# Two dense layers behind local and strided attention on one core: score blocks of 32 queries, and probabilities transposed two blocks at a time

## The chip, the cores and the metric

One core of a Trainium2 chip runs the whole program in one launch. The metric is the device time of one execution in microseconds (us), lower is better. The engines are TensorE (PE in the profile, its weight loads PEld), VectorE (DVE), ScalarE (ACT), GpSimd (POOL) and SyncE (SP), which here only issues DMAs.

## What is computed

Attention of 4 batches x 8 heads with 576 positions and head size 64, then two dense layer pairs on the 2304 tokens of 512 features, all in fp32 (the dense layers as sums of rounded products):

```python
rel = pos[:, None] - pos[None, :]
mask_local = (rel >= 0) & (rel < 32)                                # heads 0..3
mask_strided = (rel >= 0) & (pos[None, :] % 32 == pos[:, None] % 32)  # heads 4..7
scores = np.where(mask, q @ k.T / 8, -1e9)
attn = softmax(scores); x = attn @ v
...
h = x @ w_in;  g = where(h >= 1, h, where(h <= -1, 0, (h + 1) ** 2 / 4));  x = g @ w_out
h = x @ w_in2; r = max(h, 0); out = (s * r * r + b) @ w_out2
```

A local query sees itself and the 31 keys before it. A strided query sees the keys before it that are a multiple of 32 away, so 18 positions of equal residue form one small causal problem.

## The kernel before

**Units.** Attention is cut into 16 units, one for each batch and pair of heads; unit `b_p` is batch b, pair p, and pairs 0 and 1 are local, 2 and 3 strided. The two heads of a pair (index `a`) lie in the two halves of the 128 partitions. A unit loads q and k (`load_qk`) and v (`load_v`), transposes q and k (`trans`), forms scores in two PSUM banks (`scores`), takes the softmax (`smax`, `sscale`, `sexp`, `ssum`, `smul`), transposes the probabilities on TensorE (`ptrans`), copies them to SBUF on ScalarE (`evac_p`), multiplies with v (`pv`) and copies the output into `xr` (`evac_o`).

**Blocks before (lines 38 and 39).** A local unit has 9 blocks of 64 queries and 96 keys, a strided one 11 blocks of 54 queries and 54 keys (three residues of 18 positions). A bank of scores first gets the mask, as a bf16 matmul with the identity over all 128 partitions; then each block adds one fp32 matmul per head, `s<-qk,qk` in the trace. `ptrans` makes one 128-row transpose per block (`p<-ident,s`). `pv` multiplies one block of one head at a time (`o<-pt,v`): weights are v, 64 columns wide; what streams are the 64 or 54 queries of the block. A strided v is loaded with 3 DMAs per head, a local one with 2 and a fill.

**Dense layers.** They make up most of TensorE's work: `h<-xh,w`, `h<-xl,w` (first layer of a pair) and `y<-g,w`, `y<-w,g` (second). Weights are split on ScalarE, VectorE and POOL into a rounded part and a rest (`c`, `wc`, `w`) as they arrive, and so is x (`x_split`: `xh`, `xl`).

**Order.** `attention_moe_moe` does not issue instructions; it records them with a planned time (`PACE`, `STARTS`, `PASSES`), and `Order.issue` replays them by its own prices, engine by engine, into the order that stands in the program: of the ready operations of an engine the one with the earliest planned time goes next. The pieces of attention thereby stand among dense matmuls. During the start it puts filler matmuls (`idle<-u`) on TensorE. The first four units (batch 0, `QUICK`) take a shorter path, load v by POOL's queue and borrow memory (tiles named `mem`); the other twelve load v by SP's queue.

Of the kernel before, what the change touches and what calls it, by code (L numbers as in the profile page):

```python
# [19 lines left out]
P = 128  # L20
# [57 lines left out]
N_MASK_L = 2 * 96  # L78
N_MASK_S = 54
N_CONST = N_MASK_L + N_MASK_S + P  # L80


def constants():

    row = np.arange(P)[:, None] % 64
    col = np.arange(96)[None, :]
    back = row - (col - 32)
    local = np.where((back >= 0) & (back < STRIDE), 0, DROP).astype(np.float32)
    first = np.where(col < 32, DROP, local).astype(np.float32)
# [3 lines left out]
    return np.ascontiguousarray(  # L93
        np.concatenate([first, local, strided, np.eye(P, dtype=np.float32)], axis=1)
    )


class Order:
# [6 lines left out]
    def __init__(self, nc):  # L105
        self.nc, self.ops, self.place, self.count, self.seen, self.first = nc, [], {}, {}, {}, {}
        self.past = set()
        self.filler = []
        self.choices, self.uses = {}, {}
        self.tiles, self.shadow = {}, bacc.Bacc("TRN2", target_bir_lowering=False, num_devices=1)  # L110
        self.now = self.earliest = 0.0
        for e in self.ENGINES:
            setattr(self, e, Order.Engine(self, e))
# [56 lines left out]
    def record(self, engine, op, args, kw):  # L170
# [191 lines left out]
def attention_moe_moe(ctx, tc, q, k, v, w1_in, w1_out, w2_in, w2_out, s_in, b_in, consts, out):  # L362
# [42 lines left out]
    class Unit:  # L405
# [31 lines left out]
        def trans(self, w):  # L437
            if w == 0:
                self.qk = [self.mem["qk"][x](f"qk{x}_{self.id}") for x in range(2)]
            o = self.qk[w][:, PAD:PAD + S]  # L440
# [19 lines left out]
        def load_v(self):  # L460
# [3 lines left out]
            for a in range(2):  # L464
                t = self.mem["v"][a](f"v{a}_{self.id}")
                if self.strided:
                    t = t[:54, :11 * D].rearrange("p (i d) -> p i d", d=D)
                    src = vh[a].rearrange("(t r) d -> t r d", r=STRIDE)
                    for r in range(3):
                        n = 11 if r < 2 else 10  # L470
                        queue.dma_start(out=t[r * NPOS:(r + 1) * NPOS, :n], in_=src[:, r:r + 3 * (n - 1) + 1:3])
                else:
                    t = t[:96, :9 * D].rearrange("p (i d) -> p i d", d=D)
                    nc.gpsimd.memset(t[:32, 0], 0.0)
                    win = vh[a]
                    ap = bass.AP(tensor=win.tensor, offset=win.offset + 32 * D, ap=[[D, 96], [64 * D, 8], [1, D]])
                    queue.dma_start(out=t[32:96, 0], in_=win[:64])
                    queue.dma_start(out=t[:, 1:], in_=ap)
                self.v.append(t)

        def scores(self):
            qt, kt = self.qk
            if not self.strided:

                nc.gpsimd.memset(kt[:, :PAD], 0.0)
            self.sp = [bank(f"s{g}_{self.id}") for g in range(2)]
            i = 0
            for g in range(2):
                n, kw = self.s_split[g], self.kw
                first = not self.strided and g == 0  # L490
                bk = self.sp[g][:, :n * kw].rearrange("p (i c) -> p i c", c=kw)
                mask = mask_s if self.strided else mask_l[:, kw:]
                if first:
                    nc.tensor.matmul(bk[:, 0], ident_b, mask_l[:, :kw], start=True, stop=False, skip_group_check=True)
                nc.tensor.matmul(
                    bk[:, first:], ident_b, mask.unsqueeze(1).to_broadcast([P, n - first, kw]), start=not first, stop=False,
                    skip_group_check=True,
                )
                for c in range(n):
                    for a in range(2):  # L500
                        r = slice(64 * a, 64 * a + 64)
                        if self.strided:
                            r0, r1 = RES * i, min(STRIDE, RES * i + RES)
                            m, kn = NPOS * (r1 - r0), NPOS * (r1 - r0)
                            of, by = [x[r, PAD + NPOS * r0:PAD + NPOS * r1] for x in (qt, kt)]
                        else:
                            m, kn = 64, self.kw
                            of, by = qt[r, PAD + 64 * i:PAD + 64 * i + 64], kt[r, 64 * i:64 * i + self.kw]
                        nc.tensor.matmul(
                            self.sp[g][64 * a:64 * a + m, c * self.kw:c * self.kw + kn], of, by,  # L510
                            start=False, stop=True, skip_group_check=True,
                        )
# [14 lines left out]

        def sscale(self):

            if self.quick:  # L530
                self.s = self.mem["s"](f"s_{self.id}")[:, :self.nb * self.kw].rearrange("p (i c) -> p i c", c=self.kw)
# [11 lines left out]
        def sexp(self):  # L543
# [4 lines left out]
            self.s = self.mem["s"](f"s_{self.id}")[:, :self.nb * self.kw].rearrange("p (i c) -> p i c", c=self.kw)  # L548
# [20 lines left out]
        def ptrans(self, part):  # L569
            i0, i1 = ((0, 8), (8, self.nb))[part]  # L570
            if part == 0:
                self.pt = [
                    self.mem["p"][x](f"pt{x}_{self.id}")[:self.kw, :n * P].rearrange("p (i c) -> p i c", c=P)
                    for x, n in enumerate((8, self.nb - 8))
                ]
            self.pb[part] = []
            for j in range(i0, i1, 4):
                n = min(4, i1 - j)
                bk = bank(f"p{j}_{self.id}")
                for i in range(j, j + n):  # L580
                    nc.tensor.transpose(bk[:self.kw, (i - j) * P:(i - j + 1) * P], self.s[:, i, :], ident)
                self.pb[part].append((j, n, bk))

        def evac_p(self, part):
            for j, n, bk in self.pb[part]:
                nc.scalar.activation(
                    out=self.pt[part][:, j - 8 * part:j - 8 * part + n],
                    in_=bk[:self.kw, :n * P].rearrange("p (i c) -> p i c", c=P),
                    func=AF.Copy,
                )  # L590

        def pv(self):
            self.ob = [bank(f"o{g}_{self.id}") for g in range(2)]
            i = 0
            for g in range(2):
                for c in range(self.o_split[g]):
                    n = min(self.qw, S - self.qw * i)
                    kn = n if self.strided else self.kw
                    for a in range(2):
                        nc.tensor.matmul(  # L600
                            self.ob[g][64 * a:64 * a + 64, c * self.qw:c * self.qw + n],
                            self.v[a][:kn, i],
                            self.pt[i // 8][:kn, i % 8, 64 * a:64 * a + n],
                            start=True, stop=True,
                        )
                    i += 1

        def evac_o(self, copy):

            x = x_raw(self.b)[:, self.pair]  # L610
            i0 = 0
            for g in range(2):
                i1 = i0 + self.o_split[g]
                c0, c1 = self.qw * i0, min(S, self.qw * i1)
                o = self.ob[g][:, :c1 - c0]
                if self.strided:
                    put(
                        self.b, copy, x.rearrange("p (t r) -> p r t", r=STRIDE)[:, c0 // NPOS:c1 // NPOS],
                        o.rearrange("p (r t) -> p r t", t=NPOS),
                    )  # L620
                else:
                    put(self.b, copy, x[:, c0:c1], o)
                i0 = i1
# [173 lines left out]
    def room(tag, width):  # L797
# [3 lines left out]
        raw=[room("raw0", 6 * P), room("raw1", 6 * P)], qk=[room("qp0", 8 * P), room("qp1", PAD + S)], s=room("as", 864),  # L801
        p=[room("qp0", 8 * P), room("qp1", PAD + S)], v=[room("v0", 11 * D), room("v1", 11 * D)],
    )
# [134 lines left out]
```

## Time and profile before

| | us |
|---|---|
| median of 3 runs | 936.61 |
| lowest, highest | 935.33, 937.09 |
| profiled execution | 936.63 |
| its span, first to last instruction | 934.8 |
| mean granted TensorE clock | 0.995 |

| engine | busy us | share of the span |
|---|---|---|
| PE | 921.9 | 99% |
| PEld | 866.4 | 93% |
| DVE | 413.1 | 44% |
| ACT | 382.8 | 41% |
| POOL | 295.9 | 32% |

Matmuls overlap, so a row of the timeline gives the start of a group, the time to its modelled end, and its count; what a group costs is read from its start to the start of the next. An fp32 matmul of scores or values leaves two records, so counts of `s` and `o` are twice those of the program. The last attention unit ends near 360 us; the rest of the span is dense layers alone.

### The profile page before, as it was taken

How to read it: one execution, taken by the hardware profiler on the slowest of the kernel's cores; microseconds unless marked ns; L12 is line 12 of the kernel's file. 1: busy time of each engine (PE TensorE's matmuls, PEld its weight loads, DVE VectorE, ACT ScalarE, POOL GpSimd, SP SyncE). 2: the span in 40 equal slices, each digit the busy share in tenths (PEclk: the TensorE clock that was granted, in tenths of full speed). 3: DMA queues.
4: the chain of work that ended last, by engine and by line, in shares of the span. 5: the costliest groups of instructions: out<-in, count | busy, mean ns of one | idle time of the engine just before them, and what ended most of it. 6: DMA issues, size and time to landing. Idle time of an engine off the chain costs nothing.

```text
span 934.8 us, 18580 instructions
## 1 busy us (share of the span) xinstructions
PE 921.9 (99%) x7744; PEld 866.4 (93%) x7744; DVE 413.1 (44%) x659; ACT 382.8 (41%) x853; POOL 295.9 (32%) x276
## 2 busy tenths in 40 slices
PE   8989999999999999999999999999999999999998
PEld 7889999999999999999999989999889999889997
DVE  2788875433334342224369996332323232222221
ACT  2777876544444443222356554222222222222221
POOL 6166554111121212222246665222222222222221
PEclk9989999999999999999999999999999999999999
DMA  9997233322322210001375910110102010000000
GB/s 160 293 288 265 69 90 85 67 39 46 62 45 62 45 61 22 1 23 70 117 258 180 320 74 2 46 46 1 46 1 69 4 66 1 23 1 23 1 23 23
DMA packets 107495, 72.77 MB, mean 78 GB/s; under 512 B 77372, under 2 KB 94184, under 8 KB 107412
## 3 DMA queue, kind: packets, MB, share of 16 engines
q1 hardware_dynamic: 106452, 70.14, 26.4%
q0 software_dynamic: 960, 1.45, 0.9%
q8 instruction: 61, 1.00, 0.5%
q14 instruction: 22, 0.18, 0.1%
HBM read 57.93 MB, written 13.63 MB: 77 GB/s over the span
## 4 chain that ended last, share of the span: by engine, by line
PE 96%; DMA 1%; ACT 1%; SPq 1%; POOL 0%; issue 0%; DVE 0%; POOLq 0%
PE h L358 44%; PE y L358 44%; PE s L358 3%; PE o L358 2%; PE p L358 2%; DMA mem<-in_k_dram 1%; PE idle L358 1%; SPq L358 1%; PE t L358 1%; POOL w L358 0%; ACT mem L358 0%; ACT c L358 0%; DVE xl L358 0%; POOL xl L358 0%; ACT qk L358 0%
## 5 line engine op out<-in xcount | busy, mean ns | idle before, releaser
L358 PE MATMUL h<-xh,w 128*128 128x256 f32 x2304 | 436.8, 282 | 0.1
L358 PEld LDWEIGHTS h<-xh,w 128*128 128x128 f32 x2304 | 364.8, 189 | 4.6 <-ACT w L358 0.3
L358 POOL TENSOR_TENSOR g<-u,g 128x512 fp32r<-128x512 f32 x144 | 189.5, 1316 | 506.2 <-ACT g L358 211.3
L358 PE MATMUL h<-xl,w 128*128 128x256 f32 x1152 | 324.4, 282 | 0.9 <-DVE xl L358 0.9
L358 PE MATMUL y<-g,w 128*128 128x256 f32 x1728 | 223.3, 282 | 0.0
L358 PEld LDWEIGHTS h<-xl,w 128*128 128x128 f32 x1152 | 217.7, 189 | 5.0 <-DVE xl L358 1.3
L358 PE MATMUL y<-w,g 128*128 128x512 f32 x864 | 212.3, 395 | 0.0
L358 PEld LDWEIGHTS y<-g,w 128*128 128x128 f32 x1728 | 210.1, 188 | 1.5
L358 PEld LDWEIGHTS y<-w,g 128*128 128x128 f32 x864 | 157.2, 188 | 32.4
L358 DVE SCALAR_TENSOR_TENSOR u<-h,u 128x512 f32<-128x512 f32 x72 | 49.7, 691 | 253.3 <-ACT u L358 253.3
L358 ACT ACTIVATE g<-u 128x512 fp32r<-128x512 f32 x144 | 90.9, 631 | 118.3 <-DVE u L358 117.6
L358 ACT ACTIVATE u<-h 128x512 f32<-128x512 f32 x72 | 43.1, 599 | 188.2 <-PE h L358 187.0
L358 DVE TENSOR_SCALAR u<-h 128x512 f32<-128x512 f32 x72 | 49.6, 690 | 143.8 <-PE h L358 139.6
L358 POOL TENSOR_TENSOR w<-wc,w 128x512 fp32r<-128x512 f32 x64 | 84.9, 1331 | 52.8 <-ACT w L358 47.9
L358 ACT ACTIVATE u<-u,half 128x512 f32<-128x512 f32 x72 | 51.9, 721 | 113.3 <-DVE u L358 109.6
L358 DVE TENSOR_TENSOR u<-h,u 128x512 f32<-128x512 f32 x72 | 49.3, 684 | 25.2 <-ACT u L358 25.2
L358 ACT ACTIVATE w<-wc 128x512 fp32r<-128x512 f32 x64 | 40.0, 627 | 15.2 <-DVE wc L358 15.1
L358 DVE TENSOR_SCALAR c<-c 128x512 int32<-128x512 int32 x64 | 42.9, 689 | 4.5 <-ACT c L358 4.5
L358 DVE SCALAR_TENSOR_TENSOR wc<-wr,c 128x512 int32<-128x512 int32 x64 | 42.7, 675 | 3.5 <-POOL w L358 3.2
L358 DVE SCALAR_TENSOR_TENSOR c<-wr,c 128x512 int32<-128x512 int32 x64 | 43.2, 686 | 0.3
L358 ACT ACTIVATE c<-wr 128x512 f32<-128x512 f32 x64 | 39.7, 630 | 7.9 <-DMA wr<-in_moe_w_out_dram 7.7
L358 DVE TENSOR_SCALAR u<-u,sbt 128x512 f32<-128x512 f32 x72 | 42.0, 584 | 1.7
(60 smaller groups left out, 514.9 us busy)
## 6 DMA issues: line engine op xcount, KB each, us to landing
wr<-in_moe_w_in_dram SPq DMA_DIRECT2D x32, 512.0 KB
wr<-in_moe_w_out_dram SPq DMA_DIRECT2D x32, 512.0 KB
x<-o SPq DMA_DIRECT2D x34, 256.0 KB
xr<-x SPq DMA_DIRECT2D x17, 512.0 KB
out_dram<-o SPq DMA_DIRECT2D x18, 256.0 KB
v<-in_v_dram SPq DMA_DIRECT2D x12, 192.0 KB
raw<-in_q_dram SPq DMA_DIRECT2D x32, 72.0 KB
raw<-in_k_dram SPq DMA_DIRECT2D x32, 72.0 KB
```

What stands on the lines that cost most here:

```text
L358: getattr(getattr(self.nc, engine), op)(*args, **kw)
```

## The change

Local blocks of 32 queries and 64 keys: 18 of them, two per score slot (`e`), so that a slot of 64 columns holds two blocks in the two 32-partition halves of a head; the mask has 64 columns. Probabilities lie at a pitch of 64 columns in both kinds of unit (a strided slot fills its 10 spare columns and the empty twelfth slot with zeros on VectorE), and `ptrans` transposes 128 columns, two slots, at once. A slot's transposed probabilities then lie in the upper or the lower 64 partitions, and v is loaded so that it matches: `pv` multiplies slot `i + x` with rows `64 x` on, into bank `ob[x]`. In `pv` the recorded matmuls are held to the written order (`in_line`). Output leaves in three copies instead of two. Strided v takes 6 DMAs per head, local v 3, and the two fills of zeros for keys before the first are gone.

```diff
-LOCAL = dict(nb=9, qw=64, kw=96, s_split=(5, 4), o_split=(8, 1))
-STRIDED = dict(nb=11, qw=54, kw=54, s_split=(6, 5), o_split=(9, 2))
-PAD = 32
+LOCAL = dict(nb=9, kw=64, s_split=(8, 1), cut=(4, 1))
+STRIDED = dict(nb=11, kw=54, s_split=(6, 5), cut=(4, 2))
+PITCH = 64
...
+def local_block(i, e):
+    return 2 * i + 1 if e else 2 * i + 2 if i < 8 else 0
...
+        if self.in_line and self.line is not None:
+            turn.add(self.line)
+        self.line = i if self.in_line else None
...
-                    t = t[:54, :11 * D].rearrange("p (i d) -> p i d", d=D)
+                    t = t[:, :6 * D].rearrange("p (i d) -> p i d", d=D)
                     src = vh[a].rearrange("(t r) d -> t r d", r=STRIDE)
-                    for r in range(3):
-                        n = 11 if r < 2 else 10
-                        queue.dma_start(out=t[r * NPOS:(r + 1) * NPOS, :n], in_=src[:, r:r + 3 * (n - 1) + 1:3])
+                    for r in range(6):
+                        n = len(range(r, STRIDE, 6))
+                        p = 64 * (r // 3) + r % 3 * NPOS
+                        queue.dma_start(out=t[p:p + NPOS, :n], in_=src[:, r::6])
                 else:
-                    nc.gpsimd.memset(t[:32, 0], 0.0)
...
-                    queue.dma_start(out=t[32:96, 0], in_=win[:64])
-                    queue.dma_start(out=t[:, 1:], in_=ap)
+                    queue.dma_start(out=t[:, :4], in_=vh[a][:512].rearrange("(i s) d -> s i d", s=P))
+                    queue.dma_start(out=t[:, 5:], in_=vh[a][32:544].rearrange("(i s) d -> s i d", s=P))
+                    queue.dma_start(out=t[:64, 4], in_=vh[a][512:])
...
+                    o = self.sp[g][:, c * kw:(c + 1) * kw]
+                    for e in range(1 if self.strided else 2):
+                        for a in range(2):
...
+                                t = 32 * local_block(i, e)
+                                m, kn, u = 32, kw, max(0, t - 32)
+                                of, by = qt[r, t:t + m], kt[r, u:u + kn]
+                            nc.tensor.matmul(
+                                o[64 * a + 32 * e:64 * a + 32 * e + m, :kn], of, by, start=False, stop=True, skip_group_check=True,
+                            )
...
+            if self.strided:
+                nc.vector.memset(t[:, :, self.kw:], 0.0)
+                nc.vector.memset(t[:, self.nb, :self.kw], 0.0)
...
+            w = P if self.strided or part == 0 else PITCH
+            bk = self.pb[part] = bank(f"p{part}_{self.id}")[:w, :cut * P]
+            for i in range(cut):
+                nc.tensor.transpose(bk[:, i * P:(i + 1) * P], self.double[:, part * self.cut[0] + i, :w], ident)
...
+            nc.in_line = True
+            for i in range(0, self.nb, 2):
+                for a in range(2):
+                    for e in range(1 if self.strided else 2):
+                        for x in range(min(2, self.nb - i)):
+                            if self.strided:
+                                n, at, j = min(54, S - 54 * (i + x)), 27 * i, i // 2
+                                kn = n
+                            else:
+                                n, at = 32, 32 * (i + 1 - e if i < 8 else i + e)
+                                j, kn = i // 2 if e else 5 + i // 2 if i < 8 else 0, 64
+                            r, c = slice(64 * x, 64 * x + kn), 64 * a + 32 * e
+                            nc.tensor.matmul(
+                                self.ob[x][64 * a:64 * a + 64, at:at + n], self.v[a][r, j], self.pt[i // 8][r, i // 2 % 4, c:c + n],
+                                start=True, stop=True,
+                            )
+            nc.in_line = False
```

**TensorE, values of strided unit 3_2.** Before, eight matmuls of the first output bank, three dense ones, and the next eight; `v_3_2_4000` and `v_3_2_4022` are v of the two heads:

```order
L358 MATMUL p_3_2_4250<-ident,s_2_4132 54x128 x4
L358 MATMUL p_3_2_4257<-ident,s_2_4132 54x128 x3
L358 MATMUL y_0_4108<-g_2_4139,w_4_1_1097 128x256 x2
L358 MATMUL o_3_2_4264<-pt_3_2_4253,v_3_2_4000 64x54
L358 MATMUL o_3_2_4264<-pt_3_2_4253,v_3_2_4022 64x54
...
L358 MATMUL o_3_2_4264<-pt_3_2_4253,v_3_2_4000 64x54
L358 MATMUL o_3_2_4264<-pt_3_2_4253,v_3_2_4022 64x54
L358 MATMUL y_0_4108<-g_2_4139,w_5_1_1188 128x256 x3
L358 MATMUL o_3_2_4264<-pt_3_2_4253,v_3_2_4000 64x54
L358 MATMUL o_3_2_4264<-pt_3_2_4253,v_3_2_4022 64x54
```

Dense matmuls stood between the blocks there. After, all 22 follow each other; the two banks `4501` and `4503` (upper and lower rows) alternate inside a head, and these are the last of them:

```order
L370 MATMUL o_3_2_4501<-pt_3_2_4497,v_3_2_4241 64x54
L370 MATMUL o_3_2_4503<-pt_3_2_4497,v_3_2_4241 64x54
L370 MATMUL o_3_2_4501<-pt_3_2_4497,v_3_2_4298 64x54
L370 MATMUL o_3_2_4503<-pt_3_2_4497,v_3_2_4298 64x54
L370 MATMUL o_3_2_4501<-pt_3_2_4497,v_3_2_4241 64x36
L370 MATMUL o_3_2_4501<-pt_3_2_4497,v_3_2_4298 64x36
L370 MATMUL y_0_4336<-g_2_4368,w_4_1_1089 128x256
L370 MATMUL y_0_4336<-g_2_4368,w_5_1_1168 128x256 x3
```

Of the twelve units of batches 1 to 3, values stood in three pieces in nine and in one or two in the others; after the change they stand in one piece, but for 1_0, 1_1, 1_2 (one matmul ahead of the rest) and 2_2 (16 and 6).

**POOL, start, softmax sums and loads of batch 0.** Before, all v loads stand ahead of the first softmax sum (`sm`):

```order
L358 DMA mem_1_201<-in_v_dram 18x11x64 x2
L358 DMA mem_1_201<-in_v_dram 18x10x64
L358 ISA
L358 TENSOR_SCALAR sm_0_304<-sm_0_304 128x9
L358 TENSOR_SCALAR sm_1_392<-sm_1_392 128x9
L358 TENSOR_SCALAR sm_3_512<-sm_3_512 128x11
L358 TENSOR_TENSOR xl_595<-xr_543,xh_584 128x512
L358 TENSOR_SCALAR sm_2_608<-sm_2_608 128x11
L358 TENSOR_TENSOR w_0_0_603<-wc_0_0_582,w_0_0_603 128x512
```

After, loads of strided v (`v_0_3`, `mem`) stand between the sums, and the last three behind the split of the first x (`xl_705`):

```order
L370 TENSOR_SCALAR sm_0_297<-sm_0_297 128x9
L370 DMA v_0_3_199<-in_v_dram 18x5x64 x2
L370 DMA mem_0_437<-in_v_dram 18x6x64 x2
L370 TENSOR_SCALAR sm_1_442<-sm_1_442 128x9
L370 DMA mem_0_437<-in_v_dram 18x5x64 x4
L370 DMA mem_1_599<-in_v_dram 18x6x64 x2
L370 DMA mem_1_599<-in_v_dram 18x5x64
L370 TENSOR_TENSOR xl_705<-xr_607,xh_688 128x512
L370 DMA mem_1_599<-in_v_dram 18x5x64 x3
L370 TENSOR_SCALAR sm_3_527<-sm_3_527 128x11
L370 TENSOR_SCALAR sm_2_669<-sm_2_669 128x11
L370 TENSOR_TENSOR w_0_0_676<-wc_0_0_656,w_0_0_676 128x512
```

What moved: `sm_3` now comes behind `xl_705` and twelve loads, `sm_2` behind three loads more; both are sums of strided units of batch 0.

## Rows read from the trace of the kernel before

**Rows 1.** The page, chain that ended last, share by engine.
```profile
PE 96%; DMA 1%; ACT 1%; SPq 1%; POOL 0%; issue 0%; DVE 0%; POOLq 0%
```

**Rows 2.** Stretches: length, busy us (count) by engine, granted clock, DMA share, GB/s.
```profile
50.00:60.00 10.00, 8.82 (x59) 7.77 (x59) 8.80 (x13) 7.01 (x15) 5.37 (x5) 0.66 0.98 267
...
120.00:360.00 240.00, 240.00 (x2524) 229.30 (x2525) 103.93 (x166) 122.20 (x373) 57.84 (x66) 1.00 0.27 60
```

**Rows 3.** Timeline, PE, 201.7 us: start, us to modelled end, operation, out<-in, count.
```profile
201.72 2.99 PE L358 MATMUL y<-g,w 128*128 128x256 f32 x24
204.55 0.28 PE L358 MATMUL h<-xh,w 128*128 128x256 f32 x1
```

**Rows 4.** Timeline, PE, scores of a local unit.
```profile
219.28 0.38 PE L358 MATMUL s<-narrow 128*128 128x96 bf16 x2
219.59 1.04 PE L358 MATMUL s<-qk,qk 64*64 64x96 f32 x20
220.56 0.34 PE L358 MATMUL s<-narrow 128*128 128x384 bf16 x1
220.83 0.88 PE L358 MATMUL s<-qk,qk 64*64 64x96 f32 x16
221.64 0.38 PE L358 MATMUL h<-xh,w 128*128 128x256 f32 x1
```

**Rows 5.** Timeline, PE, values of units 0_3 (o<-pt,v) and 0_2 (o<-mem,mem).
```profile
46.51 0.24 PE L358 MATMUL o<-mem,mem 54*64 54x54 f32 x1
46.53 0.22 PE L358 MATMUL o<-pt,v 36*64 36x36 f32 x1
46.59 0.41 PE L358 MATMUL o<-mem,mem 54*64 54x54 f32 x8
```

**Rows 6.** Timeline, PE, transposes and values of a strided unit.
```profile
209.50 1.36 PE L358 MATMUL p<-ident,s 128*54 128x128 f32 x11
210.61 0.48 PE L358 MATMUL y<-g,w 128*128 128x256 f32 x2
211.02 0.67 PE L358 MATMUL o<-pt,v 54*64 54x54 f32 x16
211.62 0.62 PE L358 MATMUL y<-g,w 128*128 128x256 f32 x3
...
213.91 0.54 PE L358 MATMUL o<-pt,v 54*64 54x54 f32 x12
214.39 0.39 PE L358 MATMUL h<-xl,w 128*128 128x256 f32 x1
```

**Rows 7.** Timeline, PE, values of a local unit in one piece.
```profile
141.54 1.27 PE L358 MATMUL o<-pt,v 96*64 96x64 f32 x36
142.74 0.51 PE L358 MATMUL y<-g,w 128*128 128x256 f32 x2
```

**Rows 8.** Timeline, PE, values of a local unit in three pieces, first and last.
```profile
330.79 0.27 PE L358 MATMUL h<-xh,w 128*128 128x256 f32 x1
331.00 0.69 PE L358 MATMUL o<-pt,v 96*64 96x64 f32 x16
...
333.35 0.39 PE L358 MATMUL h<-xl,w 128*128 128x256 f32 x1
333.58 0.39 PE L358 MATMUL h<-xh,w 128*128 128x256 f32 x2
```

**Rows 9.** Timeline, POOL, start.
```profile
7.31 2.00 POOL L358 DMA_DIRECT2D v<-in_v_dram  x3
...
34.29 0.21 POOL L358 TENSOR_SCALAR sm<-sm 128x11 f32<-128x11 f32 x1 [5.86 <-DVE sm L358]
38.43 1.30 POOL L358 TENSOR_TENSOR xl<-xr,xh 128x512 fp32r<-128x512 f32 x1 [3.93 <-ACT xh L358]
```

**Rows 10.** DMA issues by line: count, KB each, median us to landing.
```profile
v<-in_v_dram POOLq DMA_DIRECT2D x4, 49.5 KB, 7.9
```

**Rows 11.** Timeline, PE, dense matmuls after the start.
```profile
53.09 0.58 PE L358 MATMUL h<-xl,w 128*128 128x256 f32 x1 [0.89 <-DVE xl L358]
```

More of the change, by code (lines that the diff above doesn't have):

```diff
@@ L77 @@
 U_BUFS, WC_BUFS = 3, 2
-N_MASK_L = 2 * 96
+N_MASK_L = 2 * 64
 N_MASK_S = 54
 N_CONST = N_MASK_L + N_MASK_S + P
+def local_block(i, e):
+    return 2 * i + 1 if e else 2 * i + 2 if i < 8 else 0
 def constants():
     row = np.arange(P)[:, None] % 64
-    col = np.arange(96)[None, :]
-    back = row - (col - 32)
+    col = np.arange(64)[None, :]
+    back = row % 32 - (col - 32)
     local = np.where((back >= 0) & (back < STRIDE), 0, DROP).astype(np.float32)
-    first = np.where(col < 32, DROP, local).astype(np.float32)
+    last = np.where(row < 32, np.where(row >= col, 0, DROP), local).astype(np.float32)
     c = np.arange(54)[None, :]
@@ L93, in constants @@
     return np.ascontiguousarray(
-        np.concatenate([first, local, strided, np.eye(P, dtype=np.float32)], axis=1)
+        np.concatenate([last, local, strided, np.eye(P, dtype=np.float32)], axis=1)
     )
@@ L110, in __init__ @@
         self.tiles, self.shadow = {}, bacc.Bacc("TRN2", target_bir_lowering=False, num_devices=1)
[L111 removed]
+        self.now = 0.0
+        self.in_line, self.line = False, None
         for e in self.ENGINES:
@@ L489, in scores @@
                 n, kw = self.s_split[g], self.kw
-                first = not self.strided and g == 0
                 bk = self.sp[g][:, :n * kw].rearrange("p (i c) -> p i c", c=kw)
-                mask = mask_s if self.strided else mask_l[:, kw:]
-                if first:
-                    nc.tensor.matmul(bk[:, 0], ident_b, mask_l[:, :kw], start=True, stop=False, skip_group_check=True)
+                mask = mask_s if self.strided else mask_l[:, (1 - g) * kw:(2 - g) * kw]
                 nc.tensor.matmul(
-                    bk[:, first:], ident_b, mask.unsqueeze(1).to_broadcast([P, n - first, kw]), start=not first, stop=False,
-                    skip_group_check=True,
+                    bk, ident_b, mask.unsqueeze(1).to_broadcast([P, n, kw]), start=True, stop=False, skip_group_check=True,
@@ L498, in scores @@
                 )
                 for c in range(n):
[L500 to L512, printed above, removed]
+                    o = self.sp[g][:, c * kw:(c + 1) * kw]
@@ L569, in ptrans @@
         def ptrans(self, part):
-            i0, i1 = ((0, 8), (8, self.nb))[part]
+            cut = self.cut[part]
             if part == 0:
                 self.pt = [
-                    self.mem["p"][x](f"pt{x}_{self.id}")[:self.kw, :n * P].rearrange("p (i c) -> p i c", c=P)
-                    for x, n in enumerate((8, self.nb - 8))
-                ]
[L576 to L582, printed above, removed]
@@ L584, in evac_p @@
-        def evac_p(self, part):
[L585 to L590, printed above, removed]
+                    self.mem["p"][y](f"pt{y}_{self.id}")[:, :n * P].rearrange("p (i c) -> p i c", c=P) for y, n in enumerate(self.cut)
+                ]
+            w = P if self.strided or part == 0 else PITCH
@@ L595, in pv @@
[L595 to L606, printed above, removed]
+            nc.in_line = True
@@ L608, in evac_o @@
+            nc.in_line = False
         def evac_o(self, copy):
             x = x_raw(self.b)[:, self.pair]
-            i0 = 0
-            for g in range(2):
[L613 to L623, printed above, removed]
+            if self.strided:
+                t = x.rearrange("p (t r) -> p r t", r=STRIDE)
+                for g in range(2):
+                    o = bass.AP(tensor=x.tensor, offset=x.offset + RES * g, ap=[list(x.ap[0]), [2 * RES, 5], [1, RES], [STRIDE, NPOS]])
+                    put(self.b, copy, o, self.ob[g][:, :270].rearrange("p (m e t) -> p m e t", e=RES, t=NPOS))
+                put(self.b, copy, t[:, 30:], self.ob[0][:, 270:306].rearrange("p (e t) -> p e t", t=NPOS))
+                return
```

33 lines of the change are left out of this document (22 added, 11 removed).

## The prediction

> **What bounds the kernel now.** I read the chain of waits first, then the busy time by stretches, then TensorE's timeline. The chain that ended last runs over TensorE for 96% of the span [rows 1], and from 120 to 360 us TensorE is busy without a gap while VectorE has 104 and ScalarE 122 of the 240 us [rows 2]. So after the start only what TensorE itself spends on attention counts. An ordinary 256-column matmul of the two dense layers starts every 0.118 us (24 from 201.72 to 204.55 us) [rows 3]; every small matmul is a detour from that stream and is priced by how far it pushes the next ordinary one. Twelve of the 16 units (batches 1 to 3, six local, six strided) lie in this stretch; the four of batch 0 lie in the start, where TensorE also runs filler and waits.
>
> The profiled execution took 936.63 us, of which the span is 934.8; the median of the three runs shown is 936.61, so the sum below needs no correction.
>
> **How small matmuls run.** Each fp32 matmul of scores and values leaves two records, two passes. One unit's 10 score matmuls of 96 columns take 0.97 us and 8 take 0.81 [rows 4]: 0.081 us for a pair of passes, one of each head. So the heads' passes lie side by side. That these are separate streams and not pairs in step is seen where two units meet: a pass of the next unit starts at 46.51 us, ahead of the last pass of the unit before it at 46.53 [rows 5]. Each part of the array works through its own passes and overtakes the others. For values, 16 passes take 0.60 us and 12 take 0.48 with 54 columns [rows 6], and 36 take 1.20 with 64 [rows 7]: 0.06 us a pair by each difference, at 54 and at 64 columns. What both have in common is the 64 columns of weights, so I price a values pass at 0.06 us whatever it streams, also for the new 32 columns.
>
> **Price of a detour.** A local unit's values in three pieces hold up the stream for 2.79 us with six ordinary matmuls among them (0.71), so 2.08 us [rows 8]. In one piece it is 1.20 [rows 7], plus 0.09 on the ordinary matmul ahead (330.79 to 331.00 is 0.21 instead of 0.118) and 0.11 on the one behind (333.35 to 333.58) [rows 8]: 1.40. A piece more costs (2.08 - 1.40)/2 = 0.34 us, and a single piece has 1.40 - 18 x 0.06 = 0.32 fixed.
>
> **The change, part by part.**
> - *Transposes of probabilities.* Eleven take 1.11 us [rows 6], 0.10 each. A local unit goes from 9 to 5, a strided one from 11 to 6: 6 x 0.40 + 6 x 0.50 = **-5.4**. The new ones have wider weights, but the identity that they stream stays 128 columns.
> - *Local scores.* Now 2.36 us from the first mask to the next ordinary matmul [rows 4], and 0.11 on that one: 2.47, of which 18 pairs are 1.46 and masks and switches 1.01. After, 36 matmuls of 64 columns lie on four parts of the array (two heads, two halves of 32 queries), nine each, so 18 passes of 0.081 x 64/96 = 0.054: 0.97. The masks lose 288 columns and one instruction of three, some 0.15. So 0.97 + 0.86 = 1.83, -0.64 a unit; over six units -3.8, and by the order one piece more on balance (+1 in units 1_0 and 1_1, -1 in 2_0), +0.3: **-3.5**.
> - *Values, strided.* Now 11 blocks x 2 passes x 0.06 + 0.32 + 2 x 0.34 = 2.32 in three pieces. After, 22 matmuls on four parts (two heads, upper and lower rows), at most six on one: 12 x 0.06 + 0.32 = 1.04. Four units gain 1.28; 2_2 stays in two pieces (0.94); 1_2 goes from two pieces to two (1.98 to 1.38, 0.60): **-6.7**.
> - *Values, local.* 36 matmuls instead of 18, at most ten on one part: 20 x 0.06 + 0.32 = 1.52. The four units that had three pieces gain 0.56. Units 1_0 and 1_1 (batch, pair) had one piece and get two, a lone matmul ahead: 1.86 against 1.40, +0.46 each: **-1.3**.
> - *Other engines.* ScalarE gets a third copy of the output per unit and loses one to two copies of probabilities; VectorE gets two fills per strided unit and has shorter local rows; POOL loses its fills. All of it is covered by TensorE, at 104 to 122 of 240 us [rows 2]; before 120 us the cover on VectorE is thin, but only some 2 us of the gain lie there. One thing is less covered: the values of a unit now wait in one piece for the last copy of probabilities, with 7 or 8 ordinary matmuls (0.9 us) between. If each came 0.3 us late, 12 units would give back 3.6; I take nothing and keep it for the range.
> - *Start.* The strided values of batch 0 are now loaded in 24 pieces on POOL's queue instead of 12, the local ones in 12 instead of 8. A load there takes about 0.67 us to issue [rows 9], and lands 7.9 us later [rows 10]. The last three now stand behind the split of the first x (POOL, 38.43 to 39.73 us) [rows 9], so they are issued by 41.7 and land near 49.5; the values that need them ran at 46.59 before [rows 5] and would end some 2.5 us later. Two softmax sums stand behind those loads, too: at 42 instead of 34.29 [rows 9], though fewer transposes and copies behind them regain most of that. Against it the order pulls four dense matmuls and the whole scores of unit 1_0 (1.8 us) into the gap. Net +0.7; bounds are -3 and +4, since the stretch from 50 to 60 us ran at a granted clock of 0.66, partly at 1.2 GHz [rows 2], after TensorE had sat partly idle, and that stretch may shrink or move. I take **+1**.
>
> Sum: -5.4 - 3.5 - 6.7 - 1.3 + 1 = -15.9, from 936.6: **920.7 us**.
>
> **A rule against it.** The rows show a pass that starts before an earlier instruction's last one [rows 5], and two weight loads at a time on the same rows (both heads' probabilities have the same partitions). The Trainium skill (TensorE: Matmul & The Clock Gate, Part 3, "The mechanism") says that matmuls keep program order in start and end and that weight loads overlap only when the row group differs. The trace disagrees on both; by that rule neighbours on one part would queue up, which is rival 3, 950.9.
>
> **Rivals.**
> 1. *Upper and lower rows that share columns exclude each other.* No row of before shows two such parts at once: the heads always had their own columns. Then each head's value passes run in one stream, 36 instead of 20 and 22 instead of 12: (16 + 10) x 0.06 x 6 = +9.4: **930.1**. Against it: the change writes them to two banks. The skill's tiling section (same page, "Measured speedup vs the span model") gives row packing of four a factor of 3.07; no run here has shown it.
> 2. *Never more than two streams*, scores included: 18 more passes of 0.054 in six local units, +5.8: **935.9**, no change that can be told. For it: two is all that the trace shows.
> 3. *Slower: shared columns exclude each other and block what is queued behind.* The order puts upper and lower rows of one head next to each other, so all value passes would run one by one: 72 instead of 20, 44 instead of 12, (52 + 32) x 0.06 x 6 = +30.2: **950.9**. It decides once more than about half of these passes are serial (15.9 of 30.2). Against it: the overtaking at 46.5 us.
> 4. *Nothing of it reaches the end*, because something else binds in 120 to 360 us. Rows 2 leave little room.
>
> **How the numbers follow.** Forecast 0.74, rival 1 0.12, rival 2 0.06, rival 3 0.06, rival 4 0.02. The forecast's own span is 914 (a start 3 us shorter, two or three us saved in the passes' gaps) to 927 (start +4, late copies). With rival 1 and its spread the range is 914 to 931.5, which leaves out most of rivals 2 to 4 and both tails. A measurement here tells about 0.2%, 1.9 us: the forecast, nearly all of rival 1 and a little of rival 2 are faster, 0.85; most of rival 2 and 4 is the same, 0.06; rival 3 and a bad start slower, 0.09.
>
> **What would show it.** Right: in the timeline a local unit's values in one piece of some 1.3 us for 72 records, a strided one's 44 in some 0.8, scores of 64 records under 1 us; ordinary matmuls still at 0.118; the last dense stretch (after the last unit) as long as before but starting some 16 us earlier. Rival 1: 72 records in over 2.1 us. Rival 2: 64 score records in 1.7. Rival 3: 72 in over 4. Start wrong: the first uninterrupted dense matmuls, 53.09 us before [rows 11], more than 4 us later. The forecast is wrong if the units shrink as priced and the end does not move with them.

## The result: 927.0 us, faster, and where the forecast of 920.7 lost 6

The changed kernel takes 927.01 us (median of 4 runs, 925.45 to 927.87) against 936.85 (4 runs of before on the same chip): a ratio of 0.9902, 95% interval 0.9889 to 0.9916. The forecast's side and range held (914 to 931.5); its size did not quite: 9.8 us gained where 15.9 were forecast, so that the time lies at the upper end of the forecast's own span (914 to 927).

The profiled execution took 925.45 us, its span is 923.7 (934.8 before). Two marks cut both spans into parts with the same work on TensorE (but for one dense matmul, 0.12 us, that the second mark puts into the last part of after). The first is the first second-layer group, `y<-g,w` x24: in both kernels batch 0, the scores of unit 1_0 and 72 dense matmuls lie ahead of it. The second is the end of the last unit's values. First before (timeline, PE):

```profile
65.21 2.99 PE L358 MATMUL y<-g,w 128*128 128x256 f32 x24
...
355.64 0.54 PE L358 MATMUL o<-pt,v 54*64 54x54 f32 x12
356.12 0.39 PE L358 MATMUL h<-xh,w 128*128 128x256 f32 x1
```

and after:

```profile
70.23 2.99 PE L370 MATMUL y<-g,w 128*128 128x256 f32 x24
...
342.73 0.97 PE L370 MATMUL o<-pt,v 54*64 54x54 f32 x44
343.63 0.39 PE L370 MATMUL h<-xl,w 128*128 128x256 f32 x1
```

| part | before | after | change |
|---|---|---|---|
| start, to the first mark | 65.2 | 70.2 | +5.0 |
| twelve units among dense matmuls | 290.9 | 273.4 | -17.5 |
| dense layers alone, to the end of the span | 578.7 | 580.1 | +1.4 |
| span | 934.8 | 923.7 | -11.1 |

So the units gave a little more than forecast (-16.9 without the start); the start took 5.0 and not 1, and 1.4 were lost in a part that the change does not touch. The first two lines are not independent: in e1 below, whose start ends earlier, the units take 277.4 us between the marks and not 273.4.

**The units.** Scores of a local unit, values of a local and of a strided one (timeline of after, PE; they answer to [rows 4], [rows 6] and [rows 7, 8]):

```profile
216.78 0.39 PE L370 MATMUL s<-narrow 128*128 128x512 bf16 x1
217.10 1.10 PE L370 MATMUL s<-qk,qk 64*32 64x64 f32 x64
218.13 0.20 PE L370 MATMUL s<-narrow 128*128 128x64 bf16 x1
218.26 0.32 PE L370 MATMUL s<-qk,qk 64*32 64x64 f32 x8
218.51 0.38 PE L370 MATMUL h<-xh,w 128*128 128x256 f32 x1
...
230.30 1.38 PE L370 MATMUL o<-pt,v 64*64 64x32 f32 x72
231.61 0.51 PE L370 MATMUL y<-g,w 128*128 128x256 f32 x2
...
300.86 0.82 PE L370 MATMUL p<-ident,s 128*128 128x128 f32 x6
301.43 1.07 PE L370 MATMUL y<-g,w 128*128 128x256 f32 x7
302.44 0.96 PE L370 MATMUL o<-pt,v 54*64 54x54 f32 x44
303.32 1.45 PE L370 MATMUL y<-g,w 128*128 128x256 f32 x10
```

Read from start to start: 64 score records hold the stream for 1.03 us (217.10 to 218.13), 72 values records for 1.31, 44 for 0.88, six transposes for 0.57. With 36 instructions on four parts of the array, 1.31 us means that four passes run side by side (one part after another, the same 72 records take 4.11 us in e10). That is what the forecast needed, and it stands against rivals 1 to 3 (72 records in over 2.1 us; 64 score records in 1.7; 72 in over 4).

**Where TensorE's time stands now.** The page's chain of waits by engine answers to [rows 1]; "issue" is time in which an engine waited for nothing that the profile shows:

```profile
PE 95%; DMA 2%; DVE 1%; issue 1%; POOL 1%; ACT 0%; POOLq 0%; DVEq 0%; ACTq 0%
```

Stretches of after (length, busy us and count of PE, PEld, DVE, ACT, POOL, granted clock, DMA share, GB/s); the last two lines answer to [rows 2]:

```profile
38.30:41.60 3.30, 3.30 (x18) 3.24 (x17) 3.14 (x7) 3.09 (x8) 1.19 (x1) 0.50 1.33 194
48.50:62.10 13.60, 12.44 (x180) 9.82 (x178) 9.34 (x15) 11.47 (x25) 7.64 (x7) 0.50 1.06 372
...
50.00:60.00 10.00, 8.84 (x141) 7.16 (x143) 6.69 (x11) 8.71 (x20) 5.56 (x5) 0.50 1.06 373
...
120.00:360.00 240.00, 240.00 (x2989) 233.16 (x2989) 109.27 (x183) 118.64 (x379) 60.33 (x54) 1.00 0.28 63
```

From 120 to 360 us TensorE still has no gap, and VectorE and ScalarE are covered as before. In the start the clock stands at its lower level (1.2 of 2.4 GHz) from 38.3 to 41.6 and from 48.5 to 62.1 us, the second time after TensorE had been busy for 6.73 of the 10 us from 40 to 50. Before, it did so for 3.4 us from 17.4 us on, and here:

```profile
51.60:58.30 6.70, 5.81 (x27) 5.36 (x27) 6.70 (x9) 3.71 (x9) 2.57 (x2) 0.50 1.00 242
```

**What makes the start late.** VectorE, POOL and TensorE of after, from their timelines (POOL answers to [rows 9], 62.38 on TensorE to [rows 11]), and the last values of 0_2 before:

```profile
29.95 0.76 DVE L370 TENSOR_REDUCE sm<-s 128x11 f32<-128x594 f32 x1
37.57 0.77 DVE L370 TENSOR_REDUCE sm<-mem 128x11 f32<-128x594 f32 x1 [3.38 <-ACT mem L370]
44.88 1.22 DVE L370 TENSOR_TENSOR s<-s,mx 128x594 f32<-128x594 f32 x1
46.02 1.84 DVE L370 TENSOR_TENSOR mem<-mem,mx 128x594 f32<-128x594 f32 x1
```
```profile
25.92 4.42 POOL L370 DMA_DIRECT2D mem<-in_v_dram  x7
40.41 1.31 POOL L370 TENSOR_TENSOR xl<-xr,xh 128x512 fp32r<-128x512 f32 x1 [10.06 <-ACT xh L370]
41.66 1.88 POOL L370 DMA_DIRECT2D mem<-in_v_dram  x3
43.63 0.49 POOL L370 TENSOR_SCALAR sm<-sm 128x11 f32<-128x11 f32 x2
44.20 3.02 POOL L370 TENSOR_TENSOR w<-wc,w 128x512 fp32r<-128x512 f32 x2
```
```profile
45.52 0.51 PE L370 MATMUL h<-xh,w 128*128 128x256 f32 x2 [2.08 <-POOL w L370]
48.01 0.65 PE L370 MATMUL p<-ident,mem 128*128 128x128 f32 x4 [1.20 <-DVE mem L370]
55.67 1.31 PE L370 MATMUL o<-mem,mem 54*64 54x54 f32 x38
62.38 0.39 PE L370 MATMUL h<-xl,w 128*128 128x256 f32 x1
```
```profile
46.59 1.49 PE L358 MATMUL o<-mem,mem 54*64 54x54 f32 x43
```

VectorE has unit 0_3's sums at 30.71 us and 0_2's at 38.34. POOL, which must add 1e-9 to them, does so at 43.63: in its program order they stand behind the split of the first x (`xl`), for which it sits idle 10.06 us, and behind three v loads that could have gone out in that time. Before, 0_3's sums went through POOL at 34.29 [rows 9], 0.1 us after VectorE had them. POOL's first split of weights (`w`) stands behind them as well, at 44.20 us and not at 40.12 as before, and TensorE waits 2.08 us for it. The values of 0_2 need the last loads, and their second piece starts at 55.67 us, where before all of them were done by 48.1. It waits for nothing there (no bracket): the three loads, out by 43.5, land 6.3 us later by the median of their issues, and the piece simply stands behind eleven transposes of unit 1_0 and six dense matmuls, where `Order.issue` had put it by its own prices.

### The profile page after: what moved, and what is told of

The parts are those of the page before. It is cut to its first block, busy times and chain, and to the rows that moved or that the text cites. A ratio compares the mean times of both kernels' runs of the same rounds, so it can differ in the third digit from the quotient of the medians.

```text
span 923.7 us, 19660 instructions
## 1 busy us (share of the span) xinstructions
PE 908.5 (98%) x8254; PEld 856.1 (93%) x8254; DVE 413.9 (45%) x675; ACT 373.6 (40%) x853; POOL 306.2 (33%) x268
## 4 chain that ended last, share of the span: by engine, by line
PE 95%; DMA 2%; DVE 1%; issue 1%; POOL 1%; ACT 0%; POOLq 0%; DVEq 0%; ACTq 0%
PE y L370 44%; PE h L370 44%; PE s L370 3%; PE o L370 2%; PE p L370 1%; DMA v<-in_v_dram 1%; DMA raw<-in_k_dram 1%; DMA mem<-in_v_dram 1%; PE t L370 1%; DVE c L370 0%; PE idle L370 0%; POOL mem L370 0%; DVE mem L370 0%; DVE wc L370 0%; POOL v L370 0%
```

## The experiments

Four questions: did the units gain what was priced (e1, e10); which part of batch 0 makes the start late (e2 to e4, e7, e8); is it the number of loads or something else in the new form (e5, e6, e9); and can the start be had back (e11, e12). "First mark", "units' end" (the second mark) and "rest" (the span behind it) are those of the profiled execution. Ratios are to before as it ran beside each kernel, with a median of 935.2 us for e1 to e4, 934.6 for e5 to e8 and 935.3 for e9 to e12.

| run | loads of v on POOL, batch 0 | median us | ratio to before, 95% | first mark | units' end | rest |
|---|---|---|---|---|---|---|
| before | 20 | 936.9 | | 65.2 | 356.1 | 578.7 |
| after | 36 | 927.0 | 0.9902 (0.9889 to 0.9916) | 70.2 | 343.6 | 580.1 |
| e5, after again | 36 | 927.5 | 0.9916 (0.9895 to 0.9938) | 73.1 | 346.4 | 580.1 |
| e1, batch 0 old | 20 | 920.4 | 0.9849 (0.9826 to 0.9871) | 61.3 | 338.7 | 578.8 |
| e7, strided of batch 0 old | 24 | 921.8 | 0.9861 (0.9840 to 0.9881) | 65.7 | 342.0 | 579.7 |
| e11, 12 loads to SP | 24 | 922.6 | 0.9860 (0.9838 to 0.9882) | 64.1* | 342.7 | 579.2 |
| e8, local of batch 0 old | 32 | 927.1 | 0.9912 (0.9893 to 0.9932) | 65.3* | 343.6 | 582.1 |
| e6, sums on VectorE | 36 | 929.3 | 0.9941 (0.9921 to 0.9960) | 72.2 | 349.4 | 579.5 |
| e9, as e7 with loads halved | 36 | 929.6 | 0.9933 (0.9916 to 0.9950) | 73.1* | 348.1 | 580.3 |
| e12, as e2, one filler more | 0 | 932.7 | 0.9967 (0.9951 to 0.9982) | 61.2* | 347.8 | 584.2 |
| e4, local alone | 24 | 932.7 | 0.9972 (0.9957 to 0.9987) | 65.7 | 352.3 | 580.0 |
| e2, all loads to SP | 0 | 932.8 | 0.9974 (0.9956 to 0.9992) | 62.2* | 343.4 | 584.3 |
| e3, strided alone | 32 | 939.5 | 1.0048 (1.0032 to 1.0064) | 66.4* | 353.4 | 582.7 |
| e10, part by part | 36 | 971.9, one run | | 77.3 | 390.4 | 579.7 |

(* The scores of unit 1_0, or some of them, lie behind this mark; whole they are under 2 us.) The marks part the programs: 70.2 to 77.3 us in the five with 36 loads of v on POOL's queue, 61.2 to 66.4 in all others, with up to 32. What e2, e3, e4, e8 and e12 lose against e7, they lose nearly all behind the first mark.

**e1: new form from batch 1 on.**

```diff
-plan(Unit(b, ...), t)
+kind = Unit if b > 0 else OldUnit        # OldUnit: the methods of before
+plan(kind(b, ...), t)
```

(Cut; e1 and e8 also load a second mask, for local blocks of the new form.)

> The new form only in batches 1 to 3; the four units of batch 0 keep the form of before, so the order up to the first dense matmuls is that of before. Theory (the units behind the start gained what was priced, 16 us, and the start gave 5 of it back): the first h group ends where it did before, the mark of equal work on TensorE is back near 65.2 us, and the time is 936.9 - 16 = 920.8 us (919.5 to 922.5). Rival (the units behind the start gained only the 10 us that the total shows): 927 again, with the start as before.

920.39 us, as the theory had it. The mark, with the same work ahead of it, lies at 61.27 us, earlier even than before (one kernel's executions differ there by some us: 70.23 in after, 73.08 in e5), and the rest is that of before. At the second mark e1 is 17.5 us ahead of before and 5.0 ahead of after; beside before on its own chip it gains 14.8 us by the medians. What was missing lies in batch 0's start, and 1.3 us in the rest. Of the 9 us by which e1 passes the first mark ahead of after, 4 are given back behind it: TensorE waits 2.0 us for ScalarE and 0.4 for VectorE there, which it does not in after, and the clock stands at 0.50 for 3.4 us from 87.6 us on.

**e2: all v of batch 0 by SP's queue.** `queue = nc.gpsimd if self.quick else nc.sync` becomes `queue = nc.sync`.

> The changed kernel, with the values of batch 0 loaded on SP's queue instead of POOL's. T1 (the 36 loads on POOL's queue hold up the softmax sums and the split of x, and land late): sums of 0_2 and 0_3 back before 40 us, the first uninterrupted dense matmuls 3 to 5 us earlier than 62.4, total 922 to 924 us. T2 (TensorE's own stalls, in which it waited for nothing that the profile shows, 4.5 us of them before 37 us): they stay, 926 to 928 us.

932.8 us: neither. TensorE's own stalls shrink to 0.4 us, and the time gets worse. SP now carries v ahead of the weights; TensorE waits 2.4 us for `xh`, 1.4 for POOL's `w` and 1.1 for ScalarE's `w` instead, and the clock stands at 0.50 from 50 to 60 us. Even so the first mark comes early, and behind it TensorE waits 4.2 us, where it does not in after, so that the units end where they do in after. And the rest, the same work as ever, is 4.2 us longer than after's and 5.5 longer than before's, which is taken up in the last section. So much else moved that e2 does not tell T1 and T2 apart.

**e3 and e4: one kind of unit alone.** `doubled(b, strided)` returns `strided`, and `not strided`.

> The new form in strided units alone, local units as before, in all batches. Steady part by the priced terms: transposes -3.0, strided values -6.7, so -9.7. T1 (POOL's queue: the 24 strided loads stay): start +4 to +5, total 931.5 to 932.5 us. T2 (stalls of TensorE by the many small local matmuls at 16.9 and 34.5 us): these go, start +0 to +1, total 927 to 928 us.

> The new form in local units alone, strided units as before, in all batches. Steady part by the priced terms: transposes -2.4, scores -3.5, values -1.3, so -7.2. T1 (POOL's queue: 12 strided loads as before, 12 local ones instead of 8): start +0 to +1.5, total 929.5 to 931 us. T2 (stalls at the local scores and values stay, 3.7 us): start +3.5 to +4.5, total 933 to 934 us.

939.5 and 932.7 us. Neither theory's sum comes out: every new order moves other waits (behind 70 us, `t` and `s` of e4 wait 1.3 and 1.4 us for ScalarE), and e3's rest is 4.0 us longer. Their first marks are near that of before, so T1's late start is missing in e3, with 32 loads on POOL. They show that the parts cannot be added up: beside before on the same chip (935.2) e3 loses 4.3 us and e4 gains 2.5, together a loss of 1.8, and the whole change gains 9.8. Where e3's strided units lost their gain is open.

**e5: the changed kernel again, on the chip of e6 to e8.**

> The changed kernel unaltered, beside the next three on one chip. 0.990 of before again, mean granted clock 0.988 to 0.990 against 0.992 to 0.996 of before: every execution, not the profiled one alone, has some 10 us more at the lower clock.

927.49 us, ratio 0.9916; mean granted clock 0.986 to 0.990. The loss in the clock is in every execution.

**e6: the sums of batch 0 off POOL.**

```diff
-nc.gpsimd.tensor_scalar(out=self.sm, ...)
+eng = nc.vector if self.quick else nc.gpsimd
+eng.tensor_scalar(out=self.sm, ...)
```

> The changed kernel, with the softmax sums of batch 0 rounded up on VectorE, so that no load on POOL's queue stands ahead of them. T1a (the start is late because the sums stand behind loads): probabilities of 0_2 and 0_3 are transposed 5 us or more earlier than 46.15, the mark of equal work is back at 66 to 67 us, total 922 to 923.5 us. T1b (the start is late because the strided values themselves land late, behind 24 loads): transposes earlier, but the values of 0_2 still end near 55 us and the total stays at 925.5 to 927.5.

929.3 us. The first transposes come 4.6 us earlier, at 41.59 instead of 46.15, and the values of 0_2 are even later (timeline, PE):

```profile
58.67 1.31 PE L370 MATMUL o<-mem,mem 54*64 54x54 f32 x38
```

Two loads still stand behind `xl`, at 40.81 us, and the second piece of the values still stands behind transposes of unit 1_0, which here wait 2.7 us for VectorE. The first mark stays late, at 72.2. Freeing the sums is not enough.

**e7 and e8: batch 0's strided, or its local units, in the old form.** `doubled` returns `b > 0 or not strided`, and `b > 0 or strided`.

> The new form everywhere but in the two strided units of batch 0, which are as before: 12 strided loads on POOL's queue instead of 24. T1 (loads on POOL's queue): the start is back, the mark of equal work at 65 to 66 us, total 920.5 to 922 us. T2 (TensorE's own stalls at the local units' many small matmuls): stalls at the scores of 0_1 and the values of 0_0 remain, some 3.7 us, total 924.5 to 926.

> The new form everywhere but in the two local units of batch 0, which are as before; the 24 strided loads stay. T1: the start stays late, total 925.5 to 927. T2: no stall of TensorE's own in the start, total 921.5 to 923.

e7 takes 921.8 us, although TensorE's own stalls are there (waits of PE, first 70 us):

```profile
PE s L378 <- issue: 1.4, 1, 1.4
...
PE idle L378 <- issue: 0.8, 1, 0.8
```

They are 2.2 us here, about half of after's 4.5; e7 lies 1.4 us behind e1, which has none, and the intervals do not separate the two. What POOL shows of e7: no load and no sum stands behind `xl`.

```profile
34.10 0.20 POOL L378 TENSOR_SCALAR sm<-sm 128x11 f32<-128x11 f32 x1 [9.29 <-DVE sm L378]
38.96 0.21 POOL L378 TENSOR_SCALAR sm<-sm 128x11 f32<-128x11 f32 x1 [4.65 <-DVE sm L378]
42.16 1.30 POOL L378 TENSOR_TENSOR xl<-xr,xh 128x512 fp32r<-128x512 f32 x1 [3.00 <-ACT xh L378]
```

e8's 927.05 meets the expectation of the load theory, and its trace does not: there, too, all loads and both sums stand ahead of `xl` (sums at 33.20 and 38.26, `xl` at 38.60), the values of 0_2 are done at 51 us, and the first mark lies at 65.3. So its start is not late; between the marks it takes 278.3 us, 4.9 more than after, with 2.7 us of waits that after does not have, and its rest is 2.0 us longer than after's for the same work. Taken by the trace, 32 loads still fit ahead of `xl`, and 36 do not.

**e9: loads alone.** As e7, but each strided load of batch 0 in two; the bytes, transposes and values are those of e7. The order is not: `Order.issue` counts the loads in, and all engines get another order in the start (TensorE from its 187th matmul on).

```diff
-queue.dma_start(out=t[r * NPOS:(r + 1) * NPOS, :n], in_=src[:, r:r + 3 * (n - 1) + 1:3])
+for m0, m1 in ((0, 6), (6, n)):
+    queue.dma_start(out=t[r * NPOS:(r + 1) * NPOS, m0:m1], in_=src[:, r + 3 * m0:r + 3 * (m1 - 1) + 1:3])
```

> As the kernel with the strided units of batch 0 in the form of before (921.8 us), but each of their 12 loads on POOL's queue cut in two: 24 loads of the same bytes, and transposes, values and fills as before. T1 (the number of loads on POOL's queue makes the start late): values of 0_2 done after 50 us instead of 49.3, the softmax sums of 0_2 and 0_3 after 42 us, total 926 to 928 us. Rival (something else in the new strided form of batch 0, its fills on VectorE or its wider transposes, costs it): 921 to 923.

929.6 us, 7.8 more than e7, of which 7.4 stand at the first mark, and POOL reads like after's (timeline, POOL, and the second piece of 0_2's values on PE):

```profile
25.91 3.74 POOL L378 DMA_DIRECT2D mem<-in_v_dram  x6
30.50 0.63 POOL L378 DMA_DIRECT2D mem<-in_v_dram  x1 [0.85 <-DMA mem<-in_v_dram]
41.94 1.30 POOL L378 TENSOR_TENSOR xl<-xr,xh 128x512 fp32r<-128x512 f32 x1 [10.81 <-ACT xh L378]
43.19 1.84 POOL L378 DMA_DIRECT2D mem<-in_v_dram  x3
45.11 0.49 POOL L378 TENSOR_SCALAR sm<-sm 128x11 f32<-128x11 f32 x2
```
```profile
56.82 1.93 PE L378 MATMUL o<-mem,mem 54*64 54x54 f32 x40
```

So the number of loads on POOL's queue is the cause, and the new form of the strided units is not. By which way it acts is read from the traces, not tried one by one: the last three loads and the two sums come behind `xl`; POOL's `w` comes behind them (TensorE waits 3.3 us for it here, 2.1 in after, 3.4 in e5, nothing in e7); and TensorE's order puts transposes and dense matmuls ahead of the last values, which in e7 stood in one piece. What the queue does and what the other order does is not separated.

**e10: the same values matmuls, part by part.**

```diff
-for i in range(0, self.nb, 2):
-    for a in range(2):
-        for e in range(1 if self.strided else 2):
-            for x in range(min(2, self.nb - i)):
+for a in range(2):
+    for x in range(2):
+        for i in range(0, self.nb - x, 2):
+            for e in range(1 if self.strided else 2):
```

> The changed kernel, its values matmuls written part by part of the array (all of one head's upper rows, then its lower rows, then the other head) instead of turn by turn. If a part's queue of passes takes any number of instructions ahead, it runs as in turn: a local unit's 72 records in 1.2 us, a strided one's 44 in 0.7. If instructions start in order and a pass must find its part free, the parts run one after another: 72 x 0.06 = 4.3 us, 44 x 0.06 = 2.6 us, total about +25 us.

The parts run one after another (timeline, PE, a local unit, and the granted clock just ahead of it and just behind it):

```profile
315.57 4.17 PE L370 MATMUL o<-pt,v 64*64 64x32 f32 x72
319.68 3.78 PE L370 MATMUL y<-g,w 128*128 128x256 f32 x16
```
```profile
310.00:315.00 5.00, 5.00 (x45) 5.00 (x44) 2.48 (x6) 1.66 (x7) 1.68 (x2) 1.00 0.00 0
...
320.00:325.00 5.00, 5.00 (x25) 5.00 (x25) 2.79 (x3) 1.40 (x4) 1.29 (x1) 0.50 0.19 63
```

4.11 us for the 72 records that take 1.31 in turn, a factor of 3.1 from the order of the instructions alone. That is the second of the two mechanisms expected. The total, +45 instead of +25, has a second term: six times between 165 and 370 us, during or shortly behind such a piece, with only a quarter of the array at work, the clock falls to 0.50 for 3.4 to 6.8 us. In the whole run it stands there for some 42 us more than in after, which at half rate is worth up to 21 (an estimate); the mean granted clock is 0.968 against 0.988 to 0.990.

**e11: half of the strided loads to SP.** In `load_v`, `q = nc.sync if a else queue` for the strided loads of batch 0.

> The changed kernel in full, but of batch 0's 24 strided loads the 12 of each second head go by SP's queue; POOL's queue keeps 24 of 36 loads. T1: the start is back, the values of 0_2 done before 50 us, the mark of equal work at 65 to 66 us, total 920.5 to 922.5 us, as fast as the kernels that keep the old form in batch 0. Rival (SP's queue delays the weights behind them, as with all 36 on it): 925 to 929.

922.6 us with the new form everywhere (ratio 0.9860), inside the range of T1 but for 0.1 us. No load stands behind `xl`, and the values of 0_2 end by 50 us:

```profile
35.90 0.21 POOL L370 TENSOR_SCALAR sm<-sm 128x11 f32<-128x11 f32 x1 [7.01 <-DVE sm L370]
40.11 0.21 POOL L370 TENSOR_SCALAR sm<-sm 128x11 f32<-128x11 f32 x1 [4.00 <-DVE sm L370]
42.31 1.30 POOL L370 TENSOR_TENSOR xl<-xr,xh 128x512 fp32r<-128x512 f32 x1 [2.00 <-ACT xh L370]
```

e1, e7 and e11 cannot be told apart, their intervals cover each other; all three beat both kernels.

**e12: e2 with one filler matmul more.**

> The kernel with all values of batch 0 on SP's queue (932.8 us), with one ordinary filler matmul more at the very start and everything else in the same order. Its last dense stretch, the same work as in the other kernels, ran at 0.119 us a matmul instead of 0.117. If that pitch hangs on how many TensorE instructions stand ahead, it moves, the 1000 matmuls that took 118.5 us take 117.0 to 117.5, and the total falls to 925 to 928 us. If it hangs on something else in that program, it stays: 118.5 us, and 932 to 933.5 us.

932.65 us, and 1000 dense matmuls behind the units take 118.50 us in both: one instruction more ahead moves nothing. What the pitch goes with is told in the last section.

## Why the prediction was right, and by how much it was off

- **Units: right.** How far each group pushes the next ordinary matmul, summed over the timeline from 75 to 360 us: transposes of probabilities 11.63 to 6.08 us, -5.5 (forecast -5.4); scores 22.13 to 18.62, -3.5 (-3.5; the scores of 1_0 lie ahead of 75 us in both); values 22.35 to some 15.5, -6.9 (-8.0). Counted with the lateness of the ordinary matmul behind each piece, which the forecast's prices of scores and values include, the three are -5.9, -3.6 and -8.1, in sum the -17.5 of the marks to within 0.1. Transposes at 0.10 and the 0.06 of a values pass held; a pass of scores came out at 0.059 instead of 0.054 (64 records on four parts, 15 steps in 0.88 us), masks and switches came out cheaper.
- **Values: right.** By the forecast's own way of counting, -8.1 stands against -8.0; 0.7 of it is a wait for ScalarE's `xr` that before had and after has not. Unit 1_2 and the lone matmuls ahead of 1_0 and 1_1 were priced right in kind. "If each came 0.3 us late", the fear about the last copy of probabilities, did not come about: no wait of TensorE on that copy stands in after's trace behind 70 us.
- **Start: the step that failed.** "I take +1" measured +5.0 (7.9 in e5), beyond the bound of +4. The sign set for it came: the first uninterrupted dense matmuls start at 62.38 us, 9.3 later than before, of which some 3 are the scores of 1_0 that now stand ahead of them. The mechanism was in the text, three loads and two sums behind the split of x. Two sizes were wrong, and one wait was not in the sum. First, "fewer transposes and copies behind them regain most of that": the split that they stand behind waits for ScalarE, at 40.41 us instead of 38.43, and both units' multiplications then run one right behind the other, 1.22 and 1.84 us, with TensorE waiting 1.20 for the second. The loads also hold up POOL's split of the first weights, for which TensorE waits 2.08. Second, the low clock was taken as something that "may shrink or move". It grew: 13.6 us at 0.50 from 48.5 and 3.3 at 38.3, against 6.8 there and another 3.4 before 21 us. Another 6.8 us at half rate are worth up to 3.4 of the 5.0 (an estimate), as TensorE was busy in 12.44 of the 13.60 us. What each of these took of the 5.0 was not tried by itself.
- **Dense layers alone: a term that I did not have,** +1.4 us (last section).
- **The reading of the overtaking was too generous.** "Each part of the array works through its own passes and overtakes the others" is true over some 20 ns [rows 5]. e10 shows the limit: a pass whose part is busy holds up those behind it, even for free parts. The four streams exist because the new code deals instructions out in turn. The Trainium skill (TensorE: Matmul & The Clock Gate, Part 3, "The mechanism") states that matmuls keep program order in start; e10 agrees with that, so I set too little by it. Its factor of 3.07 for four row-packed tiles (same page, "Measured speedup vs the span model") is near the 3.1 here, which four parts of 64 rows and 64 columns gave.
- **Rivals.** 1 and 2 fell by the 1.31 and 1.03 us. Of 3 the first half fell with them: parts that share columns do not exclude each other. The second half, that a pass blocks what is queued behind it, is right, and e10 shows it for passes on one and the same part. 4 fell with the second mark, 12.5 us earlier than before.

Sum: the units -17.5, start +5.0, dense layers +1.4 make -11.1 in the profiled executions; the medians differ by 9.8 since the profiled run of after was the fastest of its four.

## What to carry to other kernels

Small matmuls that use different parts of the array run side by side only if the program deals them out in turn, so write the loop over parts innermost. When an edit raises the number of DMAs on a queue that also computes, look at what the order puts behind the queue's next long wait: here three loads and two 0.2 us sums came behind a 10 us wait, and the order with 12 loads on another queue is 4.9 us faster, more than a third of what it gains in all (e11 against e5). And look at where TensorE's clock falls: in the start of after, idle time from 40 to 50 us was followed by 13.6 us of work at 0.50.

## What the runs showed that I had not expected

**The pitch of a dense matmul goes with where its operands lie.** The same dense work behind the units took 578.7 to 584.3 us, by program: 1000 dense matmuls took 117.41 us in after and in e5 alike, 118.50 in e2 and in e12, 117.08 before, with no wait in them. The order decides which byte address in SBUF each tile gets; the addresses here are those of the built programs. Grouped by the address of the x tile minus that of the weight tile, modulo 256 bytes, the mean time from one first-layer matmul to the next (ns, and how many):

```
difference       0              32             128            160
before           119.2 (192)    117.0 (2741)   118.3 (198)
after            119.5 (393)    116.8 (1964)                  118.2 (588)
e2               119.3 (2557)                  118.5 (394)    117.5 (198)
e8               119.6 (197)                                  117.9 (2750)
e11              119.5 (198)    116.8 (2161)                  117.9 (588)
```

Of these four, 0 is the slowest in every program and 32, where it stands, the fastest, by 2.4 ns, 2%. A fifth difference, 192, stands in seven programs with some 195 matmuls each, and its mean goes from 114.9 ns in e11 to 117.8 in after: so the difference alone does not fix the pitch. Before had nearly all of its tiles at 32, after fewer, e2 nearly all at 0. It goes with the rests in the table (4000 matmuls at 1.1 ns more are 4.4 us; e8's rest is 3.4 longer than before's), and comparisons of 0.5% between orders of this kernel carry it. No run moved one tile alone, so the link is a grouping of what ran, not an experiment.

**TensorE runs dry in a crowded start.** With the local form new in batch 0 and loads on POOL, TensorE stalled up to 2 us at a time for nothing that the profile shows; waits of after, PE, first 70 us:

```profile
PE s L370 <- issue: 2.8, 2, 2.0
...
PE o L370 <- issue: 1.7, 1, 1.7
```

Before, e1, e3 and e8, with half as many instructions for these units, have none. The DMA engines are full at that time (a share of 1.12 to 1.28 from 10 to 40 us), and the stalls lie near the fetches of instructions by DMA (fetches at 15.9, 26.3 and 33.4 us, stalls from 16.9, 28.2 and 34.5). That they are waits for instructions was not tried. They alone do not make the start late: e4, e7 and e11 have 3.0, 2.2 and 2.7 us of them and pass the first mark at 65.7, 65.7 and 64.1 us, where after, with 4.5, passes it at 70.2.
